# Later transforms' arithmetic moved 200 places back in the scheduler's order of preference, on one Trainium2 core

## The chip, the cores and the metric

The kernel runs on one core of a Trainium2 chip. The metric is the device time of one execution in microseconds (us), as a median of several. The core has five engines with a queue of instructions each: TensorE (PE, with its weight loads as PEld), VectorE (DVE), ScalarE (ACT), GpSimd (POOL) and SyncE (SP), which here only issues DMAs. An engine takes its queue in order; semaphores hold an instruction until what it needs is done.

## The reference

Three stages follow each other. The first is a circular convolution along the sequence, done in the frequency domain. The other two work on each token.

```python
# x: (8, 3072, 256); filt_r, filt_i: (1537, 256)
X = np.fft.rfft(x, axis=1)
y = np.fft.irfft(X * (filt_r + 1j * filt_i)[None], n=3072, axis=1)
# spectral result goes through a token-shifted mixture
x_prev = y shifted by one token (zero first)
xk = mu_k * y + (1 - mu_k) * x_prev;  xr = mu_r * y + (1 - mu_r) * x_prev
k = np.maximum(xk @ w_k, 0)                      # 256 -> 1024
z = sigmoid(xr @ w_r) * ((k * k) @ w_v)          # 1024 -> 256
# and a maximum of three products
h = np.maximum(np.maximum(z @ w1, z @ w2), z @ w3)   # 256 -> 768, 24576 tokens
out = h @ w_out                                   # 768 -> 256
```

## The kernel before

All matrix products run as three products of float32r parts (high by high, high by low, low by high), so each operand is split in two: `split` casts the high part on ACT and subtracts it on POOL (or DVE) for the low part.

**The transform.** A 3072-point transform is done as small matrix products in three stages for each of the 8 batch rows. The first row's transform, `fft_first`, runs alone at the start. The seven later ones come from `fft(b)`, one for the next row while the main work of the present row runs:

- stage A (24 pieces): `x_load` and `z_load` load the input (tiles `xr`, `xz`), `a_diff` and `a_sum` add or subtract on DVE and split, `a_mm` multiplies by `wa_s` on PE, copies the result on ACT and stores it to DRAM;
- stage B (12 pieces): `b_load` loads the piece's weights (`wbc`), its filter values (`filt`) and the stored stage A result (`xb`), and splits `xb`; `b_mm` multiplies on PE, applies the filter with three DVE instructions and one POOL instruction on the tile `filt`, and splits that into `yh`, `yl`;
- stage C: `c_mm` multiplies `yh`, `yl` by the same `wbc` tile, copies on ACT and stores the result for `y_load`.

The tiles rotate through few buffers: three for `filt`, `xr` and `xz` together, two for `xd`, `xs`, `xb` together, three for `wbc`.

**The main work** goes over 64 chunks of 384 tokens. `kv(i)` does the products `pk`, `pv` and `pr` of one chunk; the tile `gate` takes the product of `pv` and the sigmoid on DVE and so frees the two PSUM banks of `pv`. `second(p)` does the products `pa1`, `pb1`, `pe1` (the profile and the trace's rows call them pa, pb, pe) and `po` of a pair of chunks. The weights for `pv` and for `second` don't fit and stream in from DRAM through ten buffers `ws`; `piece_of` issues each of these loads on SP, at most 8 pieces ahead of its use in the written order.

**What sets the order.** The pieces of the transform are written between those of the main work by `drive`, by weights. A scheduler with a timeline model (`schedule_with_timeline_sim=True`) then makes the queue of each engine from the written program: among instructions that it holds ready it prefers the one with the earlier place. All loads of `ws`, `xr`, `xz`, `wbc`, `filt`, `xb` and `cin` stand in one queue, SP's.

Of the kernel before, what the change touches and what calls it, by code (L numbers as in the profile page):

```python
# [197 lines left out]
def tile_spectral_moe(ctx: ExitStack, tc, x, xr, xz, filt, ones, wa, wa1, wi, wbc, wb1, wc1, filt1, filt0, mu, w_k, w_v, w_r, w1, w2, w3, w_out, out):  # L198
# [7 lines left out]
    PB = P // MC  # L206
    NCH = NM // MC
    LAG = 3
    AHEAD = 8
    DF = w_k.shape[1]  # L210
    NF = DF // P
# [37 lines left out]
    def split(hi, lo, src, lo_eng=None):  # L249
        nc.scalar.copy(hi, src)  # L250
        (lo_eng or nc.gpsimd).tensor_tensor(lo, src, hi.bitcast(F32), ALU.subtract)  # L251
# [81 lines left out]
    def piece_of(i):  # L333
        while len(loaded) < min(i + AHEAD, len(stream)):
            src, shape = stream[len(loaded)]
            t = ws.tile([P, *shape], F32R, tag="ws", name="ws")
            nc.sync.dma_start(t.bitcast(F32), src)
            loaded.append(t)
        return loaded[i]
# [60 lines left out]
    def fft(b):  # L400

        s1a = dp.tile([NM, 4, GA, C], F32, tag="s1a", name=f"s1a_{b}")
        s1b = dp.tile([NM, 4, GB, C], F32, tag="s1b", name=f"s1b_{b}")
        s2 = dp.tile([NM, 4, NG, C], F32, tag="s2", name=f"s2_{b}")
        s2_of[b] = s2
        st = {}
        pieces = []
        H = NK // 2

        def x_load(t):  # L410
            st["x", t] = fp.tile([NK, NR, C], F32, tag="filt", name="xr", bufs=3)
            nc.sync.dma_start(st["x", t], xr[b, t])

        def z_load(t):
            st["z", t] = fp.tile([NK, 2, 2, C], F32, tag="filt", name="xz", bufs=3)
            nc.sync.dma_start(st["z", t], xz[b, t])

        def a_halves(u, v):
            hi = fp.tile([NK, 2, C], F32R, tag="fhi", name="xah", bufs=3)
            lo = fp.tile([NK, 2, C], F32R, tag="flo", name="xal", bufs=3)  # L420
            split(hi, lo, v, nc.gpsimd)
            st["a", u] = hi, lo

        def a_diff(u, t):
            z = st.pop(("z", t))
            v = fp.tile([NK, 2, C], F32, tag="fin", name="xd")
            nc.vector.tensor_tensor(v, z[:, 0], z[:, 1], ALU.subtract)  # L427
            a_halves(u, v)

        def a_sum(u, t):  # L430
            v = fp.tile([NK, 2, C], F32, tag="fin", name="xs")
            for k in range(2):
                x0 = st.pop(("x", t + k))
                nc.vector.tensor_tensor(v[:, k], x0[:, 0], x0[:, 1], ALU.add)
                nc.vector.tensor_tensor(v[:, k], v[:, k], x0[:, 2], ALU.add)
            a_halves(u, v)

        def a_mm(u):
            t, k = divmod(u, 3)
            w = 0 if k == 1 else 1  # L440
            hi, lo = st.pop(("a", u))
            p = ps.tile([NK, 2, C], F32, tag="pm", name="pa")
            mm3(p, [(wa_s[:, 0, w], wa_s[:, 1, w])], [(hi, lo)])
            o = fp.tile([NK, 2, C], F32, tag="fo", name="ao")
            nc.scalar.copy(o, p)
            if w == 0:
                d = s1a[8 * t : 8 * t + 8].rearrange("(k j) r g c -> (j r g) k c", k=2)
            else:
                m = 8 * t + 2 * k
                d = s1b[m : m + 4].rearrange("(k j) r g c -> (j r g) k c", k=2)  # L450
            nc.scalar.dma_start(d, o)

        NU3 = NM // 8 * 3
        NBS = NG // 2
        for u in range(NU3 + 1):
            def pa(u=u):
                t, k = divmod(u, 3)
                if u == 0:
                    z_load(0)
                if u < NU3:  # L460
                    if k == 0:
                        x_load(2 * t)
                        x_load(2 * t + 1)
                        a_diff(u, 2 * t)
                    elif k == 1:
                        z_load(2 * t + 1)
                        a_sum(u, 2 * t)
                    else:
                        if 2 * t + 2 < NM // 4:
                            z_load(2 * t + 2)  # L470
                        a_diff(u, 2 * t + 1)
                if u >= 1:
                    a_mm(u - 1)
            pieces.append((0.69, pa))

        def b_load(s):
            w = fp.tile([NK, 4, 2, NK], F32R, tag="wbc", name="wbc", bufs=3)
            nc.sync.dma_start(w.bitcast(F32), wbc_d[s].bitcast(F32))
            f = fp.tile([NK, 2, 2, C], F32, tag="filt", name="filt", bufs=3)
            nc.sync.dma_start(f, filt[:, s])  # L480
            t = fp.tile([NK, 2, C], F32, tag="fin", name="xb")
            sv, k = (s1a, 2 * s) if 2 * s < GA else (s1b, 2 * s - GA)
            nc.sync.dma_start(t, sv.rearrange("m r g c -> (m r) g c")[:, k : k + 2, :])
            hi = fp.tile([NK, 2, C], F32R, tag="fhi", name="xbh", bufs=3)
            lo = fp.tile([NK, 2, C], F32R, tag="flo", name="xbl", bufs=3)
            split(hi, lo, t)
            st["b", s] = w, f, hi, lo

        def b_mm(s):
            w, f, hi, lo = st.pop(("b", s))  # L490
            p = ps.tile([NK, 2, C], F32, tag="pm", name="pb")
            for g in range(2):
                mm3(p[:, g], [(w[:, 0, g], w[:, 1, g])], [(hi[:, g], lo[:, g])], g > 0, True)

            fr, fi = f[:, 0], f[:, 1]
            H = NK // 2
            nc.vector.scalar_tensor_tensor(fi[:H], p[H:], -1.0, fi[:H], ALU.mult, ALU.mult)
            nc.vector.tensor_tensor(fi[H:], p[:H], fi[H:], ALU.mult)
            nc.vector.tensor_tensor(fr, p, fr, ALU.mult)
            (nc.gpsimd).tensor_tensor(fr, fr, fi, ALU.add)  # L500
            yh = fp.tile([NK, 2, C], F32R, tag="fhi", name="yh", bufs=3)
            yl = fp.tile([NK, 2, C], F32R, tag="flo", name="yl", bufs=3)
            split(yh, yl, fr)
            st["c", s] = w, yh, yl

        def c_mm(s):
            w, yh, yl = st.pop(("c", s))
            p = ps.tile([NK, 2, C], F32, tag="pm", name="pc")
            for g in range(2):
                mm3(p[:, g], [(w[:, 2, g], w[:, 3, g])], [(yh[:, g], yl[:, g])], g > 0, True)  # L510
            o = fp.tile([NK, 2, C], F32, tag="fo", name="co")
            nc.scalar.copy(o, p)
            nc.scalar.dma_start(s2.rearrange("m r g c -> (m r) g c")[:, 2 * s : 2 * s + 2, :], o)

        for s in range(NBS + 2):
            def pb(s=s):
                if s < NBS:
                    b_load(s)
                if 1 <= s <= NBS:
                    b_mm(s - 1)  # L520
            def pc(s=s):
                if s >= 2:
                    c_mm(s - 2)
            pieces.append((0.65, pb))
            if s == 0:

                pieces.append((6.0, lambda: None))
            pieces.append((0.65, pc))
        return pieces

    def fft_first(pp, jobs):
# [29 lines left out]
        def wc_load(s, q=nc.sync):  # L561
            tr = pp.tile([NK, LW, NK], F32, tag="wcr", name="wcr", bufs=2)
            q.dma_start(tr[:H], wc1[:H, s * LW : (s + 1) * LW])
            ti = pp.tile([NK, LW, NK], F32, tag="wci", name="wci", bufs=2)
            q.dma_start(ti[H:], wc1[H:, s * LW : (s + 1) * LW])
            wt[s] = (*wt[s], tr, ti)

        def w_double(s):
            _, tr, ti = wt[s]
            nc.scalar.copy(tr[H:], tr[:H])  # L570
            nc.scalar.copy(ti[:H], ti[H:])
# [162 lines left out]
    def k_mm(i, f):  # L734
# [6 lines left out]
        nc.vector.scalar_tensor_tensor(r, p, 0.0, r, ALU.max, ALU.mult)  # L741
        hi = mp.tile([P, NT], F32R, tag="khi", name="khi", bufs=LAG + 1)
        lo = mp.tile([P, NT], F32R, tag="klo", name="klo", bufs=LAG + 1)
        split(hi, lo, r, nc.vector if i == 0 or i < 4 and f % 2 else None)
# [146 lines left out]
    def kv(i, before=()):  # L891
# [14 lines left out]
        for f in range(NF):  # L906
# [4 lines left out]
            if f == 4 and direct:  # L911
                add(1.3, y_mm, i + 1)
            if f >= LAG:
                add(0.98, v_mm, i, f - LAG, at[f - LAG])
        for f in range(NF - LAG, NF):
            add(0.98, v_mm, i, f, at[f])
# [165 lines left out]
```

## Time and profile before

| | us |
|---|---|
| median of 3 runs (lowest, highest) | 3163.23 (3160.59, 3163.87) |
| profiled execution | 3161.27 |
| its span, first to last instruction | 3159.5 |
| PE busy, weight loads busy | 3080.0, 3020.4 |
| DVE, ACT, POOL busy | 1922.4, 1884.8, 1858.6 |

The span is 1.8 us less than the profiled execution's own time, which is 2.0 us under the median. Busy times are unions of the instructions' intervals; an engine's rest is idle. The mean granted TensorE clock is 0.990 of full speed.

### The profile page before, as it was taken

The page shows a single profiled execution, that of the slowest core. Times are in us where ns is not written, and L with a number is a line of the kernel's source. Part 1 is how long each engine was busy: PE and PEld are TensorE (multiplying, and loading weights), DVE is VectorE, ACT ScalarE, POOL GpSimd, SP SyncE. Part 2 cuts the span into 40 slices and gives each one's busy share as a digit, 9 for nine tenths or more (in the row PEclk, how much of TensorE's full clock was granted, in tenths as well). Part 3 has the DMA queues.
Part 4 walks back from the last instruction along what each step waited for, and adds up shares of the span by engine and source line. Part 5 has one row for each costly group of instructions (what it writes and reads, how often), then busy time and mean ns, then how long its engine had stood idle before and what let it go on. Part 6 is the DMA issues. An engine that isn't in the chain of part 4 may idle for free.

```text
span 3159.5 us, 55818 instructions
## 1 busy us (share of the span) xinstructions
PE 3080.0 (97%) x19172; PEld 3020.4 (96%) x19172; DVE 1922.4 (61%) x3050; ACT 1884.8 (60%) x3968; POOL 1858.6 (59%) x1591
## 2 busy tenths in 40 slices
PE   6799999999999999999999999999999999999998
PEld 4699999999999999999999999999999999999998
DVE  4976676556664666556655566656666566555554
ACT  5556656566565566656666556566666566555554
POOL 3545765567554676556756566556765468444443
PEclk8899999999999999999999999999999999999999
DMA  9878787667776677758767587765887567555554
GB/s 298 267 260 285 235 305 227 188 197 251 260 233 184 224 240 227 254 171 259 251 221 220 183 263 261 227 205 183 262 268 237 180 214 232 178 169 165 161 170 122
DMA packets 400951, 705.92 MB, mean 223 GB/s; under 512 B 41472, under 2 KB 153120, under 8 KB 400032
## 3 DMA queue, kind: packets, MB, share of 16 engines
q1 hardware_dynamic: 333648, 621.26, 62.1%
q10 hardware_dynamic: 64576, 72.45, 6.5%
q0 software_dynamic: 2448, 8.65, 0.8%
q8 instruction: 155, 2.54, 0.3%
q14 instruction: 124, 1.02, 0.1%
HBM read 616.35 MB, written 92.14 MB: 224 GB/s over the span
## 4 chain that ended last, share of the span: by engine, by line
PE 81%; DVE 6%; DMA 5%; POOL 3%; issue 3%; ACT 1%; ACTq 0%; SPq 0%; POOLq 0%; DVEq 0%
PE pb L225 17%; PE pk L225 15%; PE pv L225 14%; PE po L225 12%; PE pe L225 8%; PE pa L225 5%; PE pr L225 4%; PE py L225 3%; DMA ws<-wud 3%; PE pc L225 2%; DVE sc L773 1%; POOL klo L251 1%; DMA s<-e 1%; DVE xd L427 1%; POOL hh L251 1%
## 5 line engine op out<-in xcount | busy, mean ns | idle before, releaser
L225 PE MATMUL pb<-x,ws 128*128 128x384 f32 x3456 | 751.7, 337 | 10.2 <-DMA ws<-wud 7.0
L251 POOL TENSOR_TENSOR hh<-m,hh 128x384 fp32r<-128x384 f32 x384 | 409.5, 1075 | 563.5 <-ACT hh L250 481.4
L251 POOL TENSOR_TENSOR klo<-kr,khi 128x384 fp32r<-128x384 f32 x492 | 520.8, 1064 | 233.2 <-ACT khi L250 205.1
L225 PEld LDWEIGHTS pb<-x,ws 128*128 128x128 f32 x3456 | 596.1, 188 | 20.5 <-issue 6.4
L741 DVE SCALAR_TENSOR_TENSOR kr<-pk,kr 128x384 f32<-128x384 f32 x512 | 281.4, 553 | 429.7 <-ACT kr L740 427.5
L225 PE MATMUL pv<-khi,ws 128*128 128x384 f32 x2048 | 481.3, 338 | 4.9 <-ACT khi L250 4.9
L225 PE MATMUL po<-wo_hi,hh 128*128 128x256 f32 x2304 | 481.4, 282 | 3.3 <-ACT hh L250 2.6
L250 ACT CAST khi<-kr 128x384 fp32r<-128x384 f32 x512 | 261.9, 513 | 226.8 <-DVE kr L741 191.9
L225 PEld LDWEIGHTS po<-wo_hi,hh 128*128 128x128 f32 x2304 | 391.1, 189 | 5.0 <-ACT hh L250 3.4
L225 PE MATMUL pe<-x,ws 128*128 128x384 f32 x1728 | 387.8, 338 | 3.5 <-DVE m L848 1.4
L225 PEld LDWEIGHTS pv<-khi,ws 128*128 128x128 f32 x2048 | 358.9, 188 | 8.5 <-ACT khi L250 6.4
L225 PE MATMUL pk<-xh,wk_hi 128*128 128x384 f32 x1024 | 341.2, 336 | 3.8 <-ACT xh L250 3.8
L225 PE MATMUL pk<-xl,wk_hi 128*128 128x384 f32 x1024 | 343.7, 336 | 0.9 <-DVE xl L251 0.9
L225 PE MATMUL pk<-xh,wk_lo 128*128 128x384 f32 x1024 | 343.3, 335 | 0.0
L225 PE MATMUL po<-wo_lo,hh 128*128 128x256 f32 x1152 | 316.8, 282 | 0.0
L740 ACT ACTIVATE kr<-pk 128x384 f32<-128x384 f32 x512 | 249.8, 489 | 108.8 <-POOL klo L251 56.8
L225 PEld LDWEIGHTS pe<-x,ws 128*128 128x128 f32 x1728 | 297.4, 188 | 8.8 <-DVE sc L855 3.1
L225 PE MATMUL pv<-klo,ws 128*128 128x384 f32 x1024 | 298.6, 338 | 2.4 <-DVE klo L251 1.3
L856 DVE TENSOR_TENSOR m<-sc,m 128x384 f32<-128x384 f32 x384 | 293.9, 768 | 8.4
L251 POOL TENSOR_TENSOR xl<-xm,xh 128x768 fp32r<-128x768 f32 x126 | 234.9, 1880 | 70.3 <-ACT xh L250 70.2
L250 ACT CAST hh<-m 128x384 fp32r<-128x384 f32 x384 | 192.6, 514 | 123.5 <-DVE m L856 85.6
L809 ACT COPY v<-pb 128x384 f32<-128x384 f32 x288 | 138.3, 480 | 188.8 <-PE pb L225 181.4
(134 smaller groups left out, 6143.1 us busy)
## 6 DMA issues: line engine op xcount, KB each, us to landing
ws<-wud SPq DMA_DIRECT2D x864, 256.0 KB, 3.8
ws<-wvd SPq DMA_DIRECT2D x512, 256.0 KB, 3.7
wbc<-wbcd SPq DMA_DIRECT2D x84, 512.0 KB, 5.5
filt<-in_filt SPq DMA_DIRECT2D x84, 512.0 KB, 4.3
ws<-wud SPq DMA_DIRECT2D x288, 128.0 KB, 3.7
xz<-in_xz SPq DMA_DIRECT2D x56, 512.0 KB, 5.2
cin<-s SPq DMA_DIRECT2D x64, 384.0 KB, 4.1
out_dram<-osb ACTq DMA_DIRECT2D x192, 128.0 KB, 2.9
```

What stands on the lines that cost most here:

```text
L225: nc.tensor.matmul(o, lhsT=wgt, rhs=rhs, start=start, stop=stop, skip_group_check=more)
L250: nc.scalar.copy(hi, src)
L251: (lo_eng or nc.gpsimd).tensor_tensor(lo, src, hi.bitcast(F32), ALU.subtract)
L427: nc.vector.tensor_tensor(v, z[:, 0], z[:, 1], ALU.subtract)
L740: nc.scalar.activation(r, p, AF.Relu)
L741: nc.vector.scalar_tensor_tensor(r, p, 0.0, r, ALU.max, ALU.mult)
L773: eng.tensor_tensor(t, a, b, ALU.subtract)
L809: nc.scalar.copy(st[to], st[of])
L856: nc.vector.tensor_tensor(m, c, m, ALU.max)
```

## The change

Five functions of the later transforms, `a_diff`, `a_sum`, `a_mm`, `b_mm` and `c_mm`, and the split in `b_load`, are wrapped so that each instruction that they issue gets a place 200 further back in the scheduler's preference. The loads `x_load`, `z_load` and those in `b_load` keep their place. `a_mm` and `c_mm` also issue their stores inside the wrapper. No instruction is added or taken away.

```diff
+    YIELD = 200
@@ in fft(b)
+        def yielding(fn):
+            def run(*a):
+                with tc.high_priority(offset=-YIELD):
+                    fn(*a)
+
+            return run
...
+        @yielding
         def a_diff(u, t):
...
+        @yielding
         def a_sum(u, t):
...
+        @yielding
         def a_mm(u):
...
-            split(hi, lo, t)
+            yielding(split)(hi, lo, t)
...
+        @yielding
         def b_mm(s):
...
+        @yielding
         def c_mm(s):
```

What the scheduler makes of it shows in the queues. The first is SP's, in the fourth row's main work, where `second` begins beside stage B; `ws_...` are streamed weights, and the number after the underscore names the tile. Before:

```order
L337 DMA ws_12806<-wud2_80 128x512
L478 DMA wbc_12877<-wbcd4_97 128x1024
L480 DMA filt_13067<-in_filt 128x1024
L337 DMA ws_12818<-wud1_79 128x256
L337 DMA ws_12829<-wud2_80 128x512
L483 DMA xb_13256<-s1b_3_10202 128x512
L337 DMA ws_12845<-wud1_79 128x512
L337 DMA ws_12852<-wud3_81 128x512
```

And now, where the same functions stand at lines 338, 490, 492 and 495:

```order
L490 DMA wbc_12877<-wbcd4_97 128x1024
L338 DMA ws_12780<-wud1_79 128x512
L338 DMA ws_12788<-wud0_78 128x512
L338 DMA ws_12806<-wud2_80 128x512
L338 DMA ws_12818<-wud1_79 128x256
L492 DMA filt_13067<-in_filt 128x1024
L338 DMA ws_12829<-wud2_80 128x512
L338 DMA ws_12845<-wud1_79 128x512
L338 DMA ws_12852<-wud3_81 128x512
L338 DMA ws_12864<-wud2_80 128x256
L495 DMA xb_13256<-s1b_3_10202 128x512
```

`filt_13067` has moved behind one more weight load, `wbc_12877` ahead of three, and `xb_13256` behind three, `ws_12852` among them.

The second is DVE's queue at the same place: `kr` and `gate` end the products of `kv`, `m` belongs to `second`, and the three instructions on `filt` are the transform's. Before:

```order
L741 SCALAR_TENSOR_TENSOR kr_12765<-pk_12758,kr_12765 128x384
L762 TENSOR_TENSOR gate_12574<-pv_12657,gate_12574 128x384
L762 TENSOR_TENSOR gate_12574<-pv_12658,gate_12574 128x384
L497 SCALAR_TENSOR_TENSOR filt_12705<-pb_12887,filt_12705 64x512
L498 TENSOR_TENSOR filt_12705<-pb_12887,filt_12705 64x512
L499 TENSOR_TENSOR filt_12705<-pb_12887,filt_12705 128x512
L852 TENSOR_TENSOR m_12834<-pa1_12844,m_12834 128x384
L848 TENSOR_TENSOR m_12857<-pe1_12851,v_12839 128x384
```

And now:

```order
L755 SCALAR_TENSOR_TENSOR kr_12765<-pk_12758,kr_12765 128x384
L866 TENSOR_TENSOR m_12834<-pa1_12844,m_12834 128x384
L862 TENSOR_TENSOR m_12857<-pe1_12851,v_12839 128x384
L510 SCALAR_TENSOR_TENSOR filt_12705<-pb_12887,filt_12705 64x512
L511 TENSOR_TENSOR filt_12705<-pb_12887,filt_12705 64x512
L512 TENSOR_TENSOR filt_12705<-pb_12887,filt_12705 128x512
L776 TENSOR_TENSOR gate_12574<-pv_12657,gate_12574 128x384
L776 TENSOR_TENSOR gate_12574<-pv_12658,gate_12574 128x384
```

The transform's group has gone behind two instructions of `second`, and the two of `gate` have gone behind the group. On PE the transform's products move by 0 to 30 matmuls of the main work, later or earlier; up to the first pieces of the first later transform all queues are the same.

## Rows read from the trace of the kernel before

**Rows 1.** The page, its first part: span, busy time and share of each engine.

```profile
span 3159.5 us, 55818 instructions
PE 3080.0 (97%) x19172; PEld 3020.4 (96%) x19172; DVE 1922.4 (61%) x3050; ACT 1884.8 (60%) x3968; POOL 1858.6 (59%) x1591
```

**Rows 2.** Busy time by window: PE, PEld, DVE, ACT, POOL (x instructions), clock, DMA share, GB/s.

```profile
500.00:2750.00 2250.00, 2238.41 (x14102) 2212.47 (x14101) 1375.56 (x2187) 1379.39 (x2920) 1393.29 (x1184) 1.00 0.71 226
2750.00:3100.00 350.00, 350.00 (x2194) 350.00 (x2193) 181.62 (x306) 196.46 (x424) 167.92 (x153) 1.00 0.53 161
```

**Rows 3.** PE's waits, 300 to 2750 us: releaser, us in total, times, longest.

```profile
PE pb L225 <- DMA ws<-wud: 6.5, 11, 1.2
PE pa L225 <- DMA ws<-wud: 1.7, 3, 0.7
```

**Rows 4.** PE's waits, 300 to 500 us: the first three of eight.

```profile
PE pc L225 <- DVE m L848: 1.4, 1, 1.4
PE pe L225 <- DVE m L848: 1.4, 1, 1.4
PE po L225 <- ACT hh L250: 1.0, 1, 1.0
...
```

**Rows 5.** PE's timeline, 1081 to 1088 us: start, us, what, idle before and releaser.

```profile
1084.19 1.82 PE L225 MATMUL pb<-x,ws 128*128 128x384 f32 x9 [1.09 <-DMA ws<-wud]
...
1086.89 0.68 PE L225 MATMUL pb<-x,ws 128*128 128x384 f32 x3
1087.41 0.68 PE L225 MATMUL pa<-x,ws 128*128 128x384 f32 x3
```

**Rows 6.** The chain that ended last, around 1080 us: start, us, what.

```profile
1078.66 5.39 DMA ws<-wud
1084.05 0.14 issue
```

**Rows 7.** SP's timeline, 1072 to 1083 us.

```profile
1072.63 0.32 SPq L478 DMA_DIRECT2D wbc<-wbcd  x1
1075.56 0.33 SPq L480 DMA_DIRECT2D filt<-in_filt  x1
1075.98 0.90 SPq L337 DMA_DIRECT2D ws<-wud  x2
1077.78 0.32 SPq L483 DMA_DIRECT2D xb<-s1b  x1
1078.19 4.73 SPq L337 DMA_DIRECT2D ws<-wud  x7
```

**Rows 8.** SP's own waits, 500 to 2750 us.

```profile
SPq L480 <- POOL yl L251: 73.4, 36, 3.0
SPq L483 <- POOL xbl L251: 64.7, 52, 3.0
SPq L412 <- DVE xd L427: 40.6, 16, 4.2
```

**Rows 9.** Tile filt, 500 to 2750 us: duration ns min/median/max, first and last start.

```profile
L497 DVE SCALAR_TENSOR_TENSOR filt<-pb,filt x72: 692/693/696, 657.3 to 2701.9; 64x512 f32<-64x512 f32 x72
L498 DVE TENSOR_TENSOR filt<-pb,filt x72: 683/684/687, 658.0 to 2702.6; 64x512 f32<-64x512 f32 x72
L499 DVE TENSOR_TENSOR filt<-pb,filt x72: 690/692/693, 658.7 to 2703.3; 128x512 f32<-128x512 f32 x72
```

**Rows 10.** All waits of the span: DVE's on the transform's product.

```profile
DVE filt L497 <- PE pb L225: 59.4, 40, 2.6
```

**Rows 11.** The page, DMA issues: KB each, us to landing.

```profile
ws<-wud SPq DMA_DIRECT2D x864, 256.0 KB, 3.8
```

**Rows 12.** Groups by line on ACT: busy us, mean ns, idle before.

```profile
L809 ACT COPY u<-pb 128x384 f32<-128x384 f32 x288 | 139.2, 483 | 77.7 <-PE pb L225 72.7 <-DVE m L852 2.3 <-DVE m L856 1.3
```

**Rows 13.** DVE's timeline, 1060 us: the two instructions on gate.

```profile
1059.59 1.02 DVE L762 TENSOR_TENSOR gate<-pv,gate 128x384 f32<-128x384 f32 x2 [0.44 <-PE pv L225]
```

## The prediction

> **What bounds the kernel now.** The first part of the page comes first: PE is busy 3080.0 of 3159.5 us, the other engines about 60% each [rows 1]. So the time is PE's queue plus the moments in which it stands still, and a change of order alone can only touch those moments. Most of PE's idle time lies before 200 us, where the first transform and the first chunk run; the queues there are unchanged. The windows then show what the later transforms cost: from 500 to 2750 us, with a transform beside the main work nearly all the time, PE is idle 2250 − 2238.4 = 11.6 us; from 2750 to 3100 us, with none, it is idle 0.0 us [rows 2]. PE's idle time understates a stall, since a matmul of 384 columns is drawn longer than its turn: three take 0.68 us in the timeline, yet the next three start 0.52 us after them [rows 5], so 0.16 us of each stall are covered by the drawn tail.
>
> The Trainium skill (Perfetto Trace Analysis, Identifying the Most-Contended Engine) says that the matmul row flatters a pipelined TensorE and that headroom is to be read from the weight loads. Those are busy 2212.5 of the 2250 us [rows 2], which leaves 37.5 us; by that the ceiling of a gain would be 37.5 us and not 11.6, and a sum by it could be some 26 us larger. I keep to stalls whose releaser can be named.
>
> PE's waits name the largest: from 300 to 2750 us it waited 11 + 3 = 14 times for a streamed weight load, 6.5 + 1.7 = 8.2 us [rows 3]. With the hidden tails (14 × 0.16 = 2.3 us) this is 10.5 us. The next are eight waits between 300 and 500 us, where the first later transform meets the preparation of weights, 6.6 us by the whole answer, of which three are shown [rows 4], 7.9 us with tails.
>
> **Why the weights are late.** One of the 14 can be followed to its cause. At 1084.19 us PE had stood 1.09 us for a `ws` tile [rows 5]; the chain goes back to its DMA, issued at 1078.66 us and 5.39 us under way [rows 6], slower than the median of 3.8 us [rows 11]. It was issued so late because SP's queue was held: after `wbc` at 1072.63 us nothing went out until `filt` at 1075.56 us, and `xb` at 1077.78 us held it a second time [rows 7]. What they wait for is the transform itself: `filt` loads waited 36 times for `yl` on POOL, 73.4 us in all, `xb` loads 52 times for `xbl`, 64.7 us, and input loads for `xd`, 40.6 us [rows 8]. The tile that came late is `ws_12852` of the excerpt, behind both holders.
>
> **The change part by part.** *SP's queue.* The scheduler moves a transform load to where its buffer is free in its model, and as the arithmetic that frees it is now later, `filt` and `xb` loads stand 1.2 and 1.9 weight loads later on average (101 and 157 places over 84 each). At the stalls that repeat from row to row I counted the matmuls between the one that frees the tile's buffer and the one that first uses the tile, in both orders: for `ws_12852` 34 before, 46 now; for `ws_14129`, the later start of `second` in the same row, 39 and 48; for `ws_15347`, the start beside stage A, 28 and 37. A matmul's turn is 0.52 / 3 = 0.173 us [rows 5], so each gains 9 × 0.173 = 1.6 us or more. The longest of the 14 stalls is 1.2 us [rows 3], 1.4 with its tail. What can eat this is that the holder's release is later as well. For `ws_12852` the product that feeds `yl` stands 2.1 us later in PE's queue. With the same 2.9 us hold the load would go out about 5.8 us before its use, against the 5.39 us that it took: 0.4 us to spare. `xb_13256`, which held the queue last, is now behind it. I take 85% of 10.5 us as gone, −9 us; bounds: −10.5 and 0.
>
> *PE, DVE, ACT, POOL.* The same instructions run, so the busy time is taken as unchanged; it is covered by PE being the bound. What moves is how closely an instruction follows the one that feeds it. The tightest new spot that repeats is in `second`: a `pb` group now comes 4 matmuls (0.69 us) after the group whose value ACT must copy out first, at six places. The copy takes 0.48 us [rows 12], which leaves 0.2 us for both semaphores. Bounds 0 and 0.5 us each, so 0 to +3 us; I take +1. Elsewhere the new distances lie within those that the trace of before passes without a stall.
>
> *300 to 500 us.* Eight waits of 7.9 us in all, on DVE and ACT. The queues there change by a few places. This stretch may lose its waits or get others like them: bounds −7.9 and +4, taken as 0.
>
> *The hand-over.* The last product of a transform stands 106 matmuls ahead of the first that uses its result for the next row, and 101 now, some 17 us of turns at 0.173 us; copy, store and load fit into that before, and 5 matmuls (0.9 us) don't change it. Cost 0; with the cover gone it would be a stall of that excess, seven times.
>
> **Sum.** −9 + 1 + 0 = −8 us. Against the profiled execution of 3161.27 us this is 3153.3 us; that execution lies 2.0 us under the median of the runs, so against the median I forecast 3155 us, −0.25%.
>
> **The rivals.**
> *The stalls only move.* At the start of stage B the new order worsens a distance: four `xb` loads now stand in a row, or nearly, just ahead of the first weights of `second`, and one of these, `ws_11610`, has 36 matmuls from its buffer's release to its use where it had 58. That is 6.2 us; with a hold of 3.0 us, the longest seen for `xb` [rows 8], and the median landing of 3.8 us [rows 11] a stall of 0.6 us follows, with a landing of 5.39 us 2.2 us, for one or two tiles of each of seven transforms: 4 to 15 us, say 8. This gives back the gain: 3163 us. For it speaks the count; against it that the loads there are issued before the weights' buffers are free, when SP has time.
>
> *It doesn't do what it says.* A load takes its landing time wherever it stands, and the late ones took 5.4 us and not 3.8, with transform loads just ahead of them. If each weight load is again issued right behind one, the stalls stay and the gain is 0 to 2 us: about 3162 us. Against it: DVE's and PE's queues did move, and the distances at the stalls grew by more than the stalls.
>
> *Slower: the transform blocks DVE.* In the excerpt the three `filt` instructions now stand ahead of `gate`. They take 0.69 + 0.68 + 0.69 = 2.07 us [rows 9] and waited for PE 59.4 / 40 = 1.5 us each time that they waited [rows 10]. `gate` (1.02 us for two [rows 13]) frees the banks of `pv`, and the new order has six places where PE takes such a bank 9 matmuls (1.56 us) after the last `pv` product. Were the group ahead of `gate` there, PE would stand 1.5 + 2.07 + 1.02 − 1.56 = 3.0 us; one such place in each of seven transforms is 21 us, less 8 is +13: 3176 us. It decides from five such places on (15 − 8 > 6.3 us). Against it: at these six places the queue shows only `kr` ahead of `gate`, and at the excerpt's place no PE group takes the bank within 4 us.
> The Trainium skill (PSUM — Partial Sum Buffer, Engine vs sequencer instructions) states that the queues of VectorE, ScalarE and GpSimdE are strictly first in, first out. By that rule a delayed transform instruction delays all arithmetic behind it, which speaks against yielding by preference alone; the trace agrees, in that DVE stood idle for it 59.4 us [rows 10].
>
> **How the numbers follow.** The forecast, most of the weight stalls gone, gets 0.55, with its own range of 3148 to 3160 us; the stalls only move 0.22; no effect 0.15; DVE blocked 0.08. A measurement of this kernel tells about 0.2% (6.3 us) from no change. Of the forecast 0.46 lies beyond that and 0.09 within, so faster is 0.46, the same 0.09 + 0.22 + 0.15 = 0.46, slower 0.08. The range is 3147 to 3168 us: down to all 10.5 us plus 5.5 of the 300 to 500 us stretch gone, up to a gain that is lost with +5 us of moved stalls.
>
> **What would show it.** Right: PE's waits for `ws` between 300 and 2750 us fall from 14 to at most 4, and SP's waits at L492 (`filt`) and L495 (`xb`) hold fewer weight loads, while PE's busy time in that stretch stays and its idle time falls from 11.6 to about 4 us. Wrong: new waits of PE on ACT `u` or on DVE `gate`, new weight waits at the start of stage B, or the same 14 at the same tiles. What would break the forecast altogether is a longer hold of SP by `filt`, since its margin at `ws_12852` is only 0.4 us.

## The result: 28 us slower, and the profile after

The changed kernel takes 3191.91 us (3190.02 to 3196.16), the kernel before 3163.55 us beside it: a ratio of 1.0094, interval 1.0082 to 1.0106. The prediction was 3155 us, with 3168 as its upper bound.

The first part of the page of the changed kernel, as in [rows 1]:

```profile
span 3194.4 us, 55751 instructions
PE 3094.0 (97%) x19172; PEld 3023.4 (95%) x19172; DVE 1890.4 (59%) x3050; ACT 1883.9 (59%) x3968; POOL 1858.0 (58%) x1591
```

The instructions are the same in number. The profiled execution is the slowest of four (3196.16 us), 34.9 us over the profiled one of before. PE is busy 14.0 us longer and idle 20.9 us longer.

Busy time by window, columns as in [rows 2]; the last two rows are windows inside the first:

```profile
500.00:2750.00 2250.00, 2219.38 (x13884) 2183.99 (x13883) 1332.43 (x2162) 1355.03 (x2871) 1375.83 (x1168) 1.00 0.69 223
2780.00:3130.00 350.00, 350.00 (x2191) 349.95 (x2190) 183.79 (x310) 200.21 (x433) 168.92 (x154) 1.00 0.52 161
909.90:916.70 6.80, 5.83 (x20) 5.77 (x20) 1.58 (x3) 2.70 (x7) 1.00 (x1) 0.50 0.87 314
1295.60:1299.00 3.40, 3.40 (x14) 3.40 (x13) 1.16 (x3) 0.69 (x2) 0.25 (x1) 0.50 1.06 396
```

The loss lies where a transform runs beside the main work: from 500 to 2750 us PE is idle 30.6 us, where it was 11.6; without a transform it is idle 0.0 us in both.

PE's waits from 300 to 2750 us, the ten largest: releaser, us, times, longest. [Rows 3] and [rows 4] answer to them.

```profile
PE pb L226 <- ACT v L823: 4.8, 5, 1.0
PE pb L226 <- DMA ws<-wud: 4.7, 4, 2.1
PE pc L226 <- DVE filt L512: 4.4, 6, 1.0
PE pk L226 <- DVE kr L755: 4.3, 8, 0.7
PE pe L226 <- DVE m L862: 3.6, 2, 2.1
PE pv L226 <- POOL klo L252: 3.5, 11, 0.6
PE po L226 <- DVE sc L869: 2.8, 5, 0.9
PE po L226 <- POOL hh L252: 1.8, 5, 0.4
PE pc L226 <- ACT yh L251: 1.7, 1, 1.7
PE pv L226 <- ACT khi L251: 1.2, 2, 0.8
```

All waits of this answer sum to 37.3 us in 57 waits; before it was 16.2 us in 28. Those for weights fell from 8.2 us in 14 to 5.7 us in 6. Those between 300 and 500 us hardly changed, from 6.6 us to 8.2 us, eight times each. What is new are 43 waits of 23.4 us behind 500 us for ACT, DVE and POOL, where before there were six of 1.4 us:

```profile
PE pe L225 <- DVE sc L855: 0.8, 5, 0.2
PE pb L225 <- DVE m L852: 0.6, 1, 0.6
```

The sum of all waits grew by 37.3 − 16.2 = 21.1 us. With the tails that the timeline hides (29 more waits × 0.16 us = 4.6 us) and 4.6 us for a low TensorE clock (below) this makes 21.1 + 4.6 + 4.6 = 30.3 of the 34.9 us.

SP's own waits, as in [rows 8]:

```profile
SPq L495 <- POOL xbl L252: 67.7, 41, 4.5
SPq L492 <- POOL yl L252: 46.9, 30, 3.0
SPq L421 <- DVE xd L437: 19.6, 16, 2.1
```

The `filt` and input loads hold SP less (73.4 and 40.6 us before), the `xb` loads as long as ever (64.7).

One stall can be followed to its cause. PE's timeline of the changed kernel around 910 us, where `second` begins beside stage A:

```profile
906.40 0.69 PE L226 MATMUL pe<-x,ws 128*128 128x384 f32 x3
909.17 0.80 PE L226 MATMUL pb<-x,ws 128*128 128x384 f32 x3 [2.08 <-DMA ws<-wud]
910.93 1.33 PE L226 MATMUL pb<-x,ws 128*128 128x384 f32 x3 [0.97 <-ACT v L823]
912.06 1.16 PE L226 MATMUL pe<-x,ws 128*128 128x384 f32 x3
```

ACT's timeline beside it (ACTq is its queue, issuing a DMA):

```profile
904.98 0.62 ACT L251 CAST xah<-xd 128x512 fp32r<-128x512 f32 x1
909.20 0.37 ACTq L463 DMA_DIRECT2D s1b<-ao  x1
909.61 0.48 ACT L860 COPY m<-pb 128x384 f32<-128x384 f32 x1 [4.01 <-DMA ws<-wud]
909.99 0.51 ACT L251 CAST hh<-m 128x384 fp32r<-128x384 f32 x1
910.40 0.48 ACT L823 COPY v<-pb 128x384 f32<-128x384 f32 x1
```

And the chain that ended last there:

```profile
901.18 7.94 DMA ws<-wud
909.12 0.02 issue
909.15 0.02 ACTq L463
```

A weight load took 7.94 us. Stage A's store, one of those whose place went back, stood in ACT's queue and left it only when that load had landed, though they share no data: in the listing of the program these stores wait for one of eight DMA semaphores as well as for their copy, so for some earlier DMA; for this store it is the one that the load of these weights counts up. ACT stood 4.01 us, the copies of `m`, `hh` and `v` behind it; PE first waited 2.08 us for the weights and then, three matmuls later, 0.97 us for `v`.

The Trainium skill (PSUM — Partial Sum Buffer, Engine vs sequencer instructions) states that ScalarE's queue is strictly first in, first out. The trace agrees: the 4.01 us fell on all copies behind the store.

`v` holds PE up at four more such places, 0.96 or 0.97 us each time, always behind a store of stage A.

TensorE's clock fell after two of these stalls: from 909.9 to 916.7 us it is granted 0.50, 1.2 GHz, and three matmuls are drawn 1.16 us and not 0.69. After waits of 0.63 and 0.97 us at 1293 us it fell for 3.4 us. After a longer pair, 1.70 and 0.96 us at 2443 us, it stayed at 1.00, so the trace doesn't show when it falls. PE was busy 5.83 and 3.40 us in the two windows, of which the full clock would have saved about half, 4.6 us; in the kernel before each window of 50 us between 500 and 2750 us has the full clock, 1.00.

### The profile page after: what moved, and what is told of

It reads as the page before. It is cut to its first block, busy times and chain, and to the rows that moved or that the text cites. A ratio compares the mean times of both kernels' runs of the same rounds, so it can differ in the third digit from the quotient of the medians.

```text
span 3194.4 us, 55751 instructions
## 1 busy us (share of the span) xinstructions
PE 3094.0 (97%) x19172; PEld 3023.4 (95%) x19172; DVE 1890.4 (59%) x3050; ACT 1883.9 (59%) x3968; POOL 1858.0 (58%) x1591
## 4 chain that ended last, share of the span: by engine, by line
PE 77%; DVE 8%; DMA 5%; POOL 4%; issue 3%; ACT 2%; ACTq 0%; SPq 0%; POOLq 0%; DVEq 0%
PE pb L226 17%; PE pv L226 13%; PE pk L226 12%; PE po L226 12%; PE pe L226 8%; PE pa L226 6%; PE pr L226 4%; PE py L226 3%; DMA ws<-wud 2%; DVE sc L787 2%; PE pc L226 1%; POOL klo L252 1%; DVE x L252 1%; DMA xr<-in_xr 1%; DMA s<-e 1%
## 5 line engine op out<-in xcount | busy, mean ns | idle before, releaser
L226 PE MATMUL pv<-khi,ws 128*128 128x384 f32 x2048 | 469.6, 337 | 6.1 <-ACT khi L251 6.1
L226 PEld LDWEIGHTS po<-wo_hi,hh 128*128 128x128 f32 x2304 | 391.2, 189 | 12.1 <-DVE sc L869 4.4
L226 PE MATMUL pv<-klo,ws 128*128 128x384 f32 x1024 | 289.6, 339 | 6.1 <-POOL klo L252 3.7
L729 DVE SCALAR_TENSOR_TENSOR xm<-yt,nmu_s,xm 128x384 f32<-128x384 f32 x256 | 185.2, 763 | 118.1 <-ACT xm L728 118.1
```

The lines of the kernel that those rows point to most:

```text
L226: nc.tensor.matmul(o, lhsT=wgt, rhs=rhs, start=start, stop=stop, skip_group_check=more)
L729: nc.vector.scalar_tensor_tensor(v[:, h], yt[:, h, :, :MC], nmu_s[:, w, h : h + 1], v[:, h], ALU.mult, ALU.add)
```

## The experiments

Five theories, as the expectations number them. **1**: the store that holds ACT's queue, and the clock behind it, are the loss. **2**: the transform's VectorE and GpSimd work closes up on the block's own. **3**: any other order loses, since the order before has few waits. **4**: the gap between loads that stay and arithmetic that goes back is the loss. **5**: the loss grows with the distance.

"Rows elsewhere" is the number of TensorE rows of the kernel's order that a line by line comparison with the order before doesn't match, buffer numbers left out, of some 11,200. Each ratio is against runs of the kernel before on the same chip (medians 3161.86 to 3163.84 us). "Idle" is PE's idle time from 500 to 2750 us, 2250 less the busy time of the window's row. "Late" counts the relus of the first layer (ACT, `kr<-pk`) that start over 3 us after the last product of their group, of 384 from the second to the seventh row, counted in each trace.

| kernel | us | ratio (interval) | rows elsewhere | idle us | late |
|---|---|---|---|---|---|
| before | 3163.55 | | 0 | 11.6 | 18 |
| the change | 3191.91 | 1.0094 (1.0082 to 1.0106) | 1484 | 30.6 | 113 |
| only_a | 3164.27 | 1.0008 (0.9999 to 1.0018) | 660 | 14.6 | 44 |
| only_b | 3192.62 | 1.0100 (1.0084 to 1.0117) | 915 | 32.1 | 80 |
| only_c | 3192.41 | 1.0099 (1.0084 to 1.0115) | 834 | 35.6 | 15 |
| store_pool | 3224.76 | 1.0197 (1.0179 to 1.0215) | 1471 | 52.8 | 121 |
| hurry_200 | 3178.03 | 1.0049 (1.0033 to 1.0065) | 1240 | 26.8 | 29 |
| back_50 | 3185.65 | 1.0074 (1.0058 to 1.0090) | 1185 | 28.6 | 81 |
| b_arith | 3161.11 | 0.9997 (0.9987 to 1.0006) | 29 | 13.7 | 19 |
| b_products | 3188.80 | 1.0087 (1.0070 to 1.0104) | 904 | 34.2 | 81 |
| klo_after | 3220.86 | 1.0189 (1.0169 to 1.0210) | 1827 | 52.4 | 120 |
| klo_before | 3193.18 | 1.0094 (1.0079 to 1.0109) | 1362 | 32.6 | 91 |
| pause_5 | 3204.06 | 1.0133 (1.0118 to 1.0148) | 1679 | 43.3 | 59 |
| pause_7 | 3190.16 | 1.0083 (1.0066 to 1.0099) | 1638 | 28.9 | 116 |
| after_pause_5 | 3194.34 | 1.0099 (1.0084 to 1.0114) | 1948 | 32.6 | 92 |
| after_pause_7 | 3184.17 | 1.0067 (1.0051 to 1.0084) | 1900 | 24.0 | 125 |

**The parts alone, and the store on another queue.**

The three parts are the change with the wrapper taken off elsewhere; for only_a:

```diff
-            yielding(split)(hi, lo, t)
+            split(hi, lo, t)
...
-        @yielding
         def b_mm(s):
...
-        @yielding
         def c_mm(s):
```

In only_b `b_mm` and the split in `b_load` alone are wrapped, in only_c `c_mm` alone. store_pool is the whole change with, in `a_mm`:

```diff
-            nc.scalar.dma_start(d, o)
+            nc.gpsimd.dma_start(d, o)
```

> Only the first stage of the later transforms (the sums, differences, their halves, products, copy and store) stands 200 instructions back; the middle stage's halves and products and the last stage's products keep the place that they had. Theory 1 (the first stage's store, which waits on ACT's queue for a transfer of an unrelated weight, is now issued where the weights land late, and holds the copies that TensorE waits for; TensorE's clock falls behind it): the stretch of the first stage carries 2.3 us of the 6.8 us of stall that each transform gained, so 3163 plus 10 to 16, 3173 to 3179. Theory 2 (the transform's VectorE and GpSimd work of all stages piles up beside the block's own at the change from the first to the second layer): 3166 to 3172, since the first stage brings only part of it. Theory 3 (any new order loses what the old one had been fitted to, whichever part moves): about +20 from each part alone, 3180 to 3190.

> Only the middle stage (halves of the loaded block, its products, the products with the filter and their halves) stands 200 instructions back. Theory 1: no first-stage store is moved, so the first stage's stalls stay as before; what the stretch of the middle and last stages gained (2.9 us per transform) is shared with the last stage: 3163 plus 0 to 12. Theory 2: the VectorE and GpSimd operations of this stage are most of what piles up, so most of the loss: 3178 to 3190. Theory 3: 3180 to 3190.

> Only the last stage (its products, the copy on ACT and the store) stands 200 instructions back. Theories 1 and 2: its copy and store meet no full DMA queue and bring no VectorE or GpSimd work, so 3160 to 3168. Theory 3: 3180 to 3190.

> The whole change, but the first stage's store is issued on GpSimd's queue instead of ACT's, so that no copy on ACT stands behind its wait. Theory 1: the first stage's stalls of 2.3 us per transform and the low clock after them go, 3175 to 3182, and no wait of TensorE for v, u or pa copies of over 0.5 us is left in the first stage. Theories 2 and 3: 3188 to 3196, the first stage's stalls stay or move, and GpSimd's queue is held by the store instead.

Stage A, whose store held ACT, costs nothing alone, 3164.27 us; its trace hardly has the stall (0.5 us of waits for `v`, in two), so this run doesn't price it. But stages B and C cost the whole loss each with stage A where it was, 3192.6 and 3192.4 us, and do not add up. Theory 1 falls as the cause; its stall is only one of many. Taking the store off ACT made it 33 us worse, 3224.76 us, but 580 TensorE rows moved with it, so that run shows little about the store itself. The last stage alone has waits that the whole change has not; PE's waits of only_c, 300 to 2750 us:

```profile
PE pb L226 <- DMA wbc<-wbcd: 16.7, 8, 2.6
PE pe L226 <- DVE m L858: 10.0, 7, 2.7
```

SP's timeline of only_c, and PE's, around 1536 us:

```profile
1534.66 0.32 SPq L487 DMA_DIRECT2D wbc<-wbcd  x1
1535.08 0.37 SPq L338 DMA_DIRECT2D ws<-wvd  x1
1536.76 0.32 SPq L487 DMA_DIRECT2D wbc<-wbcd  x1
```

```profile
1536.45 0.28 PE L226 MATMUL pc<-yh,wbc 128*128 128x256 f32 x1
```

Stage C later, with stage B in its place, holds the three `wbc` buffers: the second load goes out right behind a last product that reads one, and PE then waits up to 2.6 us for it. No run gives `wbc` a fourth buffer, so this reading isn't tested by itself.

**The distance, the direction, and the loads with it.**

In loads_too `x_load`, `z_load` and the whole of `b_load` are wrapped as well; the other three change the number, here hurry_200, with 50 and 400 in back_50 and back_400.

```diff
+        @yielding
         def b_load(s):
```

```diff
-    YIELD = 200
+    YIELD = -200
```

> The loads of the later transforms stand 200 instructions back as well, so that the whole transform moves as one. Theory 4 (the loss comes from the gap that the change opens between loads that stay and arithmetic that goes back: buffers of filt, wbc and xb are held longer, and the transform's stages close up): the gap is gone, 3160 to 3168. Theory 3 (each part lands beside other work than the order was fitted to, and meets whatever is tight there): 3180 to 3200, with stalls at places of its own.

> The same parts as in the change stand 200 instructions forward instead of back. Theory 4: arithmetic follows its loads sooner, no buffer is held longer, 3155 to 3165. Theory 3: 3180 to 3200 as well, since this too is another order. A third theory, that late arithmetic is what costs (theory 5, by the distance): below 3163, or 3163.

> The same parts 50 instructions back. Theory 5 (a loss in proportion to the distance): a quarter of 28, 3168 to 3172. Theory 3: not in proportion, anywhere from 3163 to 3195.

> The same parts 400 instructions back. Theory 5: twice 28, 3210 to 3225. Theory 3: no more than the change itself, 3180 to 3200. Theory 4: the gap between loads and arithmetic is wider, 3195 to 3225.

loads_too took 3188.26 us (ratio 1.0080, 1.0062 to 1.0098), back_400 3190.16 us (1.0085, 1.0069 to 1.0101). Neither is a test of theories 4 or 5: with buffer numbers left out, the queues of all five engines are the same as in the changed kernel, row for row. They are repeats of it, and put its order at 3188 to 3192 us. In both, PE waits for `v` five times and 4.8 us again, and the clock falls once between 500 and 2750 us, for 3.4 us, and not twice. They show that 200 places are already as far back as it goes. back_50 has four fifths of the loss at a quarter of the distance, with waits at other places, so the loss is not in proportion; and 200 places forward loses 15 us. Theory 5 falls. Theory 4 expected 3155 to 3165 us from going forward, which didn't come; the run that was to close its gap, loads_too, left the gap as it was.

**Which half of the middle stage; GpSimd relieved.** By then the traces had sharpened theory 2. Busy time by window of the kernel before, and of the changed one 15.7 us later, at the same place in the fourth row (the end of a first layer; columns as in [rows 2], POOL's busy time is the fifth number behind the length):

```profile
1515.20:1531.20 16.00, 16.00 (x108) 16.00 (x108) 10.97 (x14) 11.37 (x23) 13.57 (x11) 1.00 0.73 233
1531.20:1553.20 22.00, 22.00 (x134) 22.00 (x133) 13.65 (x20) 14.78 (x32) 18.62 (x17) 1.00 0.59 173
```

```profile
1530.90:1546.90 16.00, 16.00 (x111) 16.00 (x110) 6.26 (x12) 10.87 (x23) 7.76 (x8) 1.00 0.74 222
1546.90:1568.90 22.00, 21.08 (x127) 20.44 (x126) 15.44 (x23) 12.12 (x27) 20.17 (x17) 1.00 0.59 190
```

POOL had 13.57 us to do in the first 16 us and has 7.76 now, then 20.17 of 22 us; PE, which never stood still, is idle 0.92 us. The late relus are of this place and two like it.

Of the wrapped functions only those of the middle stage are left, and of `b_mm` only a part stands in the wrapper: in b_arith all that follows the matmuls, with the split in `b_load`; in b_products the matmuls alone, as in this cut:

```diff
-        @yielding
         def b_mm(s):
...
-            for g in range(2):
-                mm3(p[:, g], [(w[:, 0, g], w[:, 1, g])], [(hi[:, g], lo[:, g])], g > 0, True)
+            with tc.high_priority(offset=-YIELD):
+                for g in range(2):
+                    mm3(p[:, g], [(w[:, 0, g], w[:, 1, g])], [(hi[:, g], lo[:, g])], g > 0, True)
```

klo_after and klo_before change one line of `k_mm`:

```diff
-        split(hi, lo, r, nc.vector if i == 0 or i < 4 and f % 2 else None)
+        split(hi, lo, r, nc.vector if i == 0 or f % 2 else None)
```

> Of the middle stage only the halves of the loaded block, the products with the filter and their halves (ACT, VectorE and GpSimd) stand 200 instructions back; its matmuls keep their place. Theory 2, as the traces now sharpen it (the change takes GpSimd work out of the stretch where GpSimd has time, 280 to 296 us into a row, into the change from the first layer to the second behind it, where the block's own halves queue on GpSimd, so that relu on ACT waits for a buffer and TensorE for a bank): this part alone carries it, 3180 to 3195, and relu starts over 3 us after its products in 60 or more of 384 cases (18 in the kernel before, 113 in the changed one, 80 with the whole middle stage back). Theory 3 (any new order costs, wherever): 3175 to 3195, with no such link to relu.

> Of the middle stage only the matmuls stand 200 instructions back; the halves and the products with the filter keep their place, though those behind the matmuls can't start sooner than these. Theory 2: less GpSimd work moves, 3165 to 3180, with fewer than 50 late relus. Theory 3: 3175 to 3195.

> The whole change, and every second low half of the first layer's squares is made on VectorE instead of GpSimd in all rows (in the kernel as changed only up to the fourth block). Some 16 us per pair of blocks leave GpSimd. Theory 2: GpSimd's queue is what holds relu at the changes of layer, so most of the loss comes back, 3165 to 3178, and late relus fall below 50. Theory 3: this is one more order, 3180 to 3200.

> The same low halves on VectorE in the kernel before. Theory 2: GpSimd holds nobody there, so nothing is gained, 3160 to 3172. Theory 3: any new order costs, 3175 to 3195.

The arithmetic alone doesn't move: 29 rows differ, and the time is that of before. The middle stage's matmuls alone carry its loss (66 rows differ from only_b, 3188.80 against 3192.62 us): what is done to a product follows the product. Giving POOL relief on VectorE made both kernels worse, by 29 us each (3220.86 from 3191.91, 3193.18 from 3163.84), against theory 2. This again moved rows, and it loads DVE, so I took POOL's work away instead.

**Half of the middle stage's GpSimd work left out; the order moved by something else.**

half_after starts from the changed kernel, half_before from the one before; `half_split` takes the place of `split` in the middle stage. The products of the second of two column groups then read the low half of the first, so PE, ACT and DVE have as many instructions as before.

```diff
+        def half_split(hi, lo, src):
+            nc.scalar.copy(hi, src)
+            nc.gpsimd.tensor_tensor(lo[:, 0], src[:, 0], hi[:, 0].bitcast(F32), ALU.subtract)
...
-            (nc.gpsimd).tensor_tensor(fr, fr, fi, ALU.add)
+            (nc.gpsimd).tensor_tensor(fr[:, 0], fr[:, 0], fi[:, 0], ALU.add)
```

pause_5 and, with 7.0, pause_7 start from the kernel before:

```diff
-                pieces.append((6.0, lambda: None))
+                pieces.append((5.0, lambda: None))
```

> The whole change, with half of the middle stage's GpSimd arithmetic left out: the low halves of the loaded block and of the filtered block, and the sum behind the filter, are made for the first of two columns of groups only (the products of the second take the low half of the first, so TensorE, ACT and VectorE do what they did). Theory 2 (the middle stage's GpSimd work, late by its matmuls, closes up on the block's low halves at the end of a first layer; relu and then TensorE wait): most of the loss comes back, 3163 to 3178, and relus that start over 3 us late fall from 113 to under 60. Theory 3 (any new order costs, wherever): 3180 to 3195, late relus as many as before.

> The same GpSimd arithmetic left out in the kernel before. Theory 2: there GpSimd holds nobody, 3155 to 3168. Theory 3: the order moves too, since the operations are shorter, 3170 to 3190.

> The kernel before, no place moved back; only the pause between the first and the middle stage of a transform weighs 5 instead of 6, so that the whole transform is spread a little differently over the blocks (some 1680 of 11265 TensorE rows stand elsewhere; the change moved 1480). Theory 3: 3175 to 3195. Theory 2: it depends on whether the middle stage's work still stands where GpSimd has time: with under 45 late relus 3160 to 3172, with over 75 3180 to 3195.

> The same with a pause of 7 (some 1640 rows stand elsewhere). Theory 3: 3175 to 3195. Theory 2: as for the pause of 5, by the count of late relus.

half_after took 3176.71 us (ratio 1.0042, 1.0027 to 1.0057), half_before 3148.91 us (0.9957, 0.9943 to 0.9972). By its time alone the first would have spoken for theory 2. Its control shows that the same edit gains 13 us in the kernel before as well; the gap between the two kernels stays, 3176.71 − 3148.91 = 27.8 us against 28.4.

That the missing GpSimd work is worth these 13 us isn't shown. Both edits change the order too, and over half of half_before's gain lies in one place, where the first later transform starts; the kernel before, and below it half_before:

```profile
385.00:490.00 105.00, 100.36 (x634) 97.99 (x633) 71.39 (x109) 62.17 (x133) 74.00 (x60) 0.98 0.83 277
385.00:490.00 105.00, 104.99 (x676) 104.38 (x675) 73.11 (x115) 65.44 (x140) 64.76 (x63) 1.00 0.84 283
```

There PE has no idle time and the full clock in half_before, and gets 42 matmuls further, by an estimate some 7 us at 0.173 us each. From 500 to 2750 us its PE is idle 14.4 us, no less than the 11.6 of before, and that of half_after 26.5 us, against 30.6: in this stretch the gap narrows from 19.0 to 12.1 us. Late relus still number 84 and 37. So theory 2 falls as the cause of most of the difference; a part of it isn't excluded. Late relus are no measure of the loss: hurry_200 has 29 and loses 15 us, only_a 44 and loses nothing, only_c 15 and loses 29.

The two pauses move no arithmetic back against its loads and lose 42 and 28 us. That is what theory 3 expected. PE's waits of pause_5, 300 to 2750 us, are again others:

```profile
PE pb L225 <- DMA ws<-wud: 16.1, 6, 3.0
PE pe L225 <- DVE gate L762: 13.1, 5, 3.3
PE pv L225 <- ACT khi L250: 12.3, 12, 1.7
```

The second of them is the prediction's slower rival, come true in another kernel. DVE's timeline of pause_5 around the third of the five waits, in which PE stood 2.82 us until 1576.51 us:

```profile
1573.17 0.69 DVE L427 TENSOR_TENSOR xd<-xz 128x512 f32<-128x512 f32 x1 [6.73 <-DMA xz<-in_xz]
1573.90 0.69 DVE L497 SCALAR_TENSOR_TENSOR filt<-pb,filt 64x512 f32<-64x512 f32 x1
1574.60 0.69 DVE L498 TENSOR_TENSOR filt<-pb,filt 64x512 f32<-64x512 f32 x1
1575.30 0.69 DVE L499 TENSOR_TENSOR filt<-pb,filt 128x512 f32<-128x512 f32 x1
1575.91 1.01 DVE L762 TENSOR_TENSOR gate<-pv,gate 128x384 f32<-128x384 f32 x2
```

The transform's four instructions stand ahead of `gate`, and the first of them waited for an input load; the rival's price was 3.0 us a place, with PE's product as what is waited for.

**The change in other orders.** Both pauses with the whole change:

```diff
+    YIELD = 200
-                pieces.append((6.0, lambda: None))
+                pieces.append((5.0, lambda: None))
```

> The whole change, and a pause of 5 instead of 6 (some 1980 of 11227 TensorE rows stand elsewhere than in the changed kernel). Theory 3, in the form that the runs so far leave (the order of the kernel before is one with unusually few waits, the changed one is a usual one): a further move of the order costs nothing on top, it comes out 3175 to 3210, as pause_5 did (3204). Rival (moving the arithmetic back has a price of its own, 28 us, whatever the order around it): 3204 plus 28, 3225 to 3240.

> The whole change, and a pause of 7 (some 1800 of 11139 TensorE rows stand elsewhere). Theory 3: 3175 to 3210 again. Rival: 3190 plus 28, 3212 to 3225.

With a pause of 5 the change takes the time from 1.0133 (1.0118 to 1.0148) to 1.0099 (1.0084 to 1.0114) of the kernel before: faster by 0.34%, the intervals don't meet. With a pause of 7 it goes from 1.0083 to 1.0067, within the intervals. So the change has no price that it keeps in another order.

Under the pause of 5 the change lets PE's idle time fall from 43.3 to 32.6 us. The waits of after_pause_5 no longer hold the 13.1 us for `gate`; the largest two are:

```profile
PE pb L226 <- DMA ws<-wud: 14.2, 12, 2.3
PE pv L226 <- ACT khi L251: 9.1, 13, 1.7
```

## Why the prediction was wrong

- **PE is the bound and only its moments of rest can change**: right. The loss is in waits and, 4.6 us of it, in the clock that follows them, which the step "busy time is taken as unchanged" had left out.
- **Weights, −9 us**: right in kind, too large. Of 14 waits 6 are left (at most 4 were forecast), 2.5 us less, with tails 2.5 + 8 × 0.16 = 3.8 us. At the place that [rows 5 to 7] follow none is left. At the start of `second` beside stage A four are, 4.7 us, since the loads there took 6.17 to 7.94 us where I counted with 5.39.
- **The `pb` group 4 matmuls behind its copy, +1 us (0 to +3)**: right. PE waits at none of the six places. The six matmuls of two groups there are drawn 1.35 us and not 1.20, which is 0.9 us for all six; from PE's timeline:

```profile
1002.65 1.35 PE L226 MATMUL pb<-x,ws 128*128 128x384 f32 x6
```

- **300 to 500 us, 0; the hand-over, 0**: right, +1.6 us at other hand-overs, and no wait of `py` in the 300 to 2750 us.
- **"Elsewhere the new distances lie within those that the trace of before passes without a stall"**: the step that failed. I put at nothing what came to 43 waits and 23.4 us. The five waits on `v` show how: from the group that is copied to the one that takes its bank there are 6 matmuls, three of `pe` and three of `pb`. The kernel before passes this distance six times without a wait, at 805 us as follows, a row of ACT's timeline and then one of PE's:

```profile
804.52 0.48 ACT L809 COPY v<-pb 128x384 f32<-128x384 f32 x1
804.84 1.72 PE L225 MATMUL pb<-x,ws 128*128 128x384 f32 x9
```

There ACT was free for the copy; in the changed kernel ACT stood behind the store, and the same 6 matmuls cost 4.8 us in five waits. A distance in matmuls is PE's side of a hand-over only. The other side, from a product to the release, doesn't keep its length when three other queues are put in a new order: relus that came over 3 us late went from 18 to 113. The one rival of that kind, at `gate`, didn't come: the changed kernel has no wait of PE for `gate`. It stood for a class of stalls, of which I priced one member.
- **The chances**: slower got 0.08 as one mechanism with one place. The runs show that it was the common case. Of 14 orders that do the whole work and move 660 rows or more, the changed one among them, 13 lose 0.49% to 1.97%, and the one that doesn't, only_a, moves the fewest. Two of the 13 are the change in other surroundings, where it gains or makes no difference against that pause alone.

What is shown, then: the change trades one order for another, and the order before has less idle time of PE, 11.6 us, than any other that was run (24.0 to 52.8 us among the 13). What stays open is why that one is so good. No single wait explains it; each order has its stalls at other hand-overs, of which only those of `v` are followed to their cause here. No version that does the whole work beats the kernel before.

## What to carry to other kernels

When a scheduler rebuilds all queues, a count of distances at the known stalls forecasts those stalls and nothing else: a distance on one engine says little where another engine gives the release. Price the new stalls too, and if the order at hand is nearly free of waits, take a loss of the size of a usual order's waits as the first case. Test a change of order in two or three surroundings (another pause, another weight) before calling it good or bad; here the same change was +0.94%, −0.34% and no difference. And give every experiment that takes work away its control in the kernel before, and see where in time the gain lies: half_after alone would have spoken for a cause that its control doesn't bear out.

## What the hardware showed beside this

- A store can hold its engine for a transfer that it has nothing to do with: 4.01 us of ACT at 909 us, until a weight load of 7.94 us landed.
- TensorE's clock fell to half for 6.8 and 3.4 us after two pairs of short waits of PE (2.08 and 0.97 us; 0.63 and 0.97 us), in a stretch where it was otherwise busy, and did not fall after a third (1.70 and 0.96 us).
